# Squared-ReLU attention and two MLPs on one core: GpSimd's elementwise work moved to VectorE, and the square taken in fp32 on ScalarE

## The chip, the cores and the metric

The kernel runs on one core of a Trainium2 chip. The metric is the device time in microseconds (us) of one execution; smaller is better.

## The reference

For each of 2 batches of 3008 rows, `scores = (z @ z.T) / S`, `attn = max(scores, 0)**2`, `out = u * (attn @ v)`, with `z` 64 wide and `u`, `v` 256 wide. The 6016 rows that result go through two MLPs of inner width 2048:

```python
h = x @ w_in                      # first MLP
P = a[0] + a[1]*h + a[2]*h**2 + a[3]*h**3
Q = 1 + abs(b[0])*abs(h) + abs(b[1])*h**2
x = (P / (Q + 1e-6)) @ w_out
h = x @ moe2_w_in                 # second MLP
out = max(0.01*h, h) @ moe2_w_out
```

All four weight matrices are float64; the kernel reads each element as two 32-bit words and builds one fp32 number from them.

## The kernel before, in words

Every product is made of three matmuls: an operand is split into a rounded copy in fp32r (the high part) and the remainder (the low part), and high x high, low x high and high x low are accumulated.

The 6016 rows lie in 12 blocks, six for each batch: five of 512 columns and one of 448 (block 5 and block 11). A block has 12 steps, each with two tiles of 128 keys, so attention is 144 steps, `t`. In step `t` TensorE does 4 matmuls of scores (`scores`, L224) and 12 of attention times V for the step two before it (`av(t - 2)`, L257); in the second step of a block 10. The score tiles `big` are two deep, the squares' tiles three (`r`, `ph`) and two (`pl`).

The order on every engine is written out by hand (`manual_schedule`), and each engine works strictly in that order. In step `t` it is:

- ScalarE: ReLU of the scores into `r` (L226), then the square of `r` rounded to fp32r, `ph` (L228).
- VectorE: `square(t)`, the square of `r` in place in fp32 (L232); `square_low(t)`, `r - ph` into `pl` (L238). The last of the 144 goes to GpSimd.
- Then the tasks of the step. `prep_v` (chunks of V, five in steps 2 to 10, six in steps 64 to 74): ScalarE rounds a chunk (L173) and the remainder is taken on GpSimd (L175), for the first chunk on VectorE. `prep_z` (steps 1, 6, 64, 68, 76): TensorE transposes, ScalarE rounds the keys (L141), VectorE takes their remainder (L142). `prep_u` (tenth step of a block): TensorE transposes (L207), ScalarE copies. At a block's end VectorE multiplies with `u` (L262).
- Weights: 32 halves, one begun every 3.4 steps, in steps 2 to 113 (`load_w`, `conv1` to `conv5`, one a step). `conv1`: ScalarE takes the absolute value of the upper word (L287) and GpSimd clamps it (L288). `conv2`, `conv3`, `conv4`: VectorE shifts and masks (L294), joins an exponent bit and the sign (L298, L299), and joins the lower word (L303). `conv5`: ScalarE rounds (L315), GpSimd takes the remainder (L316), and for the second MLP's weights SyncE stores both to DRAM (L318).

All DMAs are issued by SyncE, in order. From step 119 the first chunks of the first MLP run between the attention steps (the merged stretch, to about 612 us); after it TensorE goes through the rest of both MLPs, with no work on GpSimd.

Of the kernel before, what the change touches and what calls it, by code (L numbers as in the profile page):

```python
# [10 lines left out]
F32R = mybir.dt.float32r  # L11
I32 = mybir.dt.int32
AF = mybir.ActivationFunctionType
ALU = mybir.AluOpType
# [3 lines left out]
def f32(ap):  # L18
    return ap.bitcast(F32)
# [3 lines left out]
def squared_relu_attention_moe_moe2(  # L23
# [14 lines left out]
    pe, act, dve, pool, sp = nc.tensor, nc.scalar, nc.vector, nc.gpsimd, nc.sync  # L38
# [9 lines left out]
    NPAIR = KB // 2  # L48
# [3 lines left out]
    blocks = []  # L52
# [9 lines left out]
    def slot(i, name, dt=F32, shape=(P, 2, QB)):  # L62
        return sb.tile(list(shape), dt, tag=f"s{i}", name=name)

    def big(name):
        return ps.tile([P, 2, QB], F32, tag="big", name=name)
# [10 lines left out]
    def rtile(i, name):  # L77
        return sb.tile([P, 2, 1024], F32R, tag=f"r{i}", name=name)
# [4 lines left out]
    C0 = 1.0 + 1e-6  # L83
    LSH = 2.0 ** -63
    par = sb.tile([P, 16], F32, tag="par", name="par")
    F64_LEAST, F64_MOST = 2.0 ** -15, 122879.9921875
    lnb, exb = par[:, 12:13], par[:, 13:14]

# [24 lines left out]
    extra_t = sb.tile([P, 2, 1024], F32, tag="r2", name="extra")  # L113
# [5 lines left out]
    def key_chunk(c):  # L119
        return keys[c // 2][:, c % 2, :]  # L120
# [48 lines left out]
    def prep_v(b, c, t):  # L169
        m = rtile(3 + c, f"V{b}_{c}")  # L170
        V[b, c] = m
        tf = t.rearrange("p k d -> p (k d)")
        act.activation(m[:, 0, :], tf, AF.Copy)  # L173
        eng = pool if b or c else dve
        eng.tensor_tensor(out=m[:, 1, :], in0=tf, in1=f32(m[:, 0, :]), op=ALU.subtract)  # L175
        if c == KB // 4 - 1:
            o = 3 * D
            act.activation(m[:KTAIL, 1, o:], f32(m[:KTAIL, 0, o:]), AF.Copy)
            pool.memset(f32(m[KTAIL:, 0, o:]), 0.0)
# [33 lines left out]
    R, PH, PL = {}, {}, {}  # L213

    def scores(t):
        i, pr = divmod(t, NPAIR)
        b, q0, n = blocks[i]
        s = big(f"sc{t}")
        for e in range(2):
            kb = 2 * pr + e  # L220
            o = (kb % 8) * P
            m = key_chunk(kb // 8)[:, o : o + P]
            for h in range(2):
                pe.matmul(s[:, e, :n], m, queries[i % 2][:, h, :n], start=h == 0, stop=h == 1)  # L224
        r = (extra[0] if t % 3 == 2 else slot(t % 3, f"r{t}"))[:, :, :n]
        act.activation(r, s[:, :, :n], AF.Relu, scale=SCALE)  # L226
        ph = slot(4 + t % 3, f"ph{t}", F32R)[:, :, :n]
        act.activation(ph, r, AF.Square)  # L228
        PH[t], R[t] = ph, r

    def square(t):
        dve.tensor_tensor(out=R[t], in0=R[t], in1=R[t], op=ALU.mult)  # L232

    def square_low(t):
        r, ph = R.pop(t), PH[t]
        pl = slot(7 + t % 2, f"pl{t}", F32R)[:, :, : blocks[t // NPAIR][2]]
        eng = pool if t == NT - 1 else dve
        eng.tensor_tensor(out=pl, in0=r, in1=f32(ph), op=ALU.subtract)  # L238
        PL[t] = pl

    def av(t):
        i, pr = divmod(t, NPAIR)
        b, q0, n = blocks[i]
        if pr == 0:
            pacc[i] = acc(own_acc(i), f"oT{i}")
        a = pacc[i]
        ph, pl = PH.pop(t), PL.pop(t)
        seq = [(0, ph), (1, ph), (0, pl)]
        for si, (h, mv) in enumerate(seq):
            for e in range(2):  # L250
                kb = 2 * pr + e
                if kb == KB - 1 and si == 0:
                    continue
                vt = V[b, kb // 4]
                for j in range(2):
                    o = (kb % 4) * D + j * P
                    pe.matmul(a[:, j, :n], vt[:, h, o : o + P], mv[:, e, :],  # L257
                              start=pr == 0 and si == 0 and e == 0,
                              stop=pr == NPAIR - 1 and si == 2 and e == 1)
        if pr == NPAIR - 1:  # L260
            xt = uT.pop(i)[:, :, :n]
            dve.tensor_tensor(out=xt, in0=xt, in1=pacc.pop(i)[:, :, :n], op=ALU.mult)  # L262
            if i < NB - 1:
                at(t + DEPTH + 2, lambda: sp.dma_start(xs[i], xt))
            else:
                sp.dma_start(xs[i], xt)
# [5 lines left out]
    conv = {}  # L272

    def load_w(k):
# [7 lines left out]
            sp.dma_start(t.rearrange("p (k d) w -> p k (d w)", k=2), src[r0 : r0 + 256, :].rearrange("(k p) w -> p k w", p=P))  # L282
        conv[k] = t

    def conv1(k):
        c = slot(15, f"cvc{k}", I32)[:, 0, :]
        act.activation(f32(c), f32(conv[k][:, :, 1]), AF.Abs)  # L287
        pool.tensor_scalar(out=f32(c), in0=f32(c), scalar1=F64_LEAST, scalar2=F64_MOST, op0=ALU.max, op1=ALU.min)  # L288
        conv["c"] = c

    def conv2(k):
        c = conv["c"]
        conv["a", k] = a = extra_t[:, 1, (k % 2) * 512 : (k % 2 + 1) * 512].bitcast(I32)
        dve.tensor_scalar(out=a, in0=c, scalar1=3, scalar2=0x3FFFFFF8, op0=ALU.logical_shift_left, op1=ALU.bitwise_and)  # L294

    def conv3(k):
        c, a, raw = conv["c"], conv["a", k], conv[k]
        dve.scalar_tensor_tensor(out=a, in0=c, scalar=0x40000000, in1=a, op0=ALU.bitwise_and, op1=ALU.bitwise_or)  # L298
        dve.scalar_tensor_tensor(out=a, in0=raw[:, :, 1], scalar=-0x80000000, in1=a, op0=ALU.bitwise_and, op1=ALU.bitwise_or)  # L299

    def conv4(k):
        a, raw = conv["a", k], conv.pop(k)
        dve.scalar_tensor_tensor(out=a, in0=raw[:, :, 0], scalar=29, in1=a, op0=ALU.logical_shift_right, op1=ALU.bitwise_or)  # L303

    def conv5(k):
        kind, j, half = halves[k]
        a = conv.pop(("a", k))
        cols = slice(half * 512, (half + 1) * 512)
        if kind < 2:
            if half == 0:  # L310
                W[kind, j] = sb.tile([P, 2, 1024], F32R, tag=f"w{kind}_{j}", name=f"w{kind}_{j}")
            w = W[kind, j][:, :, cols]
        else:
            w = slot(9, f"wst{k}", F32R)
        act.activation(w[:, 0, :], f32(a), AF.Copy)  # L315
        pool.tensor_tensor(out=w[:, 1, :], in0=f32(a), in1=f32(w[:, 0, :]), op=ALU.subtract)  # L316
        if kind >= 2:
            sp.dma_start(w2s[kind, j][:, :, cols], f32(w))  # L318

# [6 lines left out]
    NT = NB * NPAIR  # L326
# [109 lines left out]
    def m1_h(c):  # L436
        i, p = divmod(c, NP)
        T[c] = {"n": blocks[i][2], "h": hidden(f"h1_{c}", 0, p, X1[i], blocks[i][2])}
# [5 lines left out]
    def m1_tb(c):  # L444
        if c % 2 and c <= MERGED:
            T[c]["t1"] = extra[1][:, :, : T[c]["n"]]
        else:
            m1_tile(c, "t1", 13 if c % 2 else 2)
        act.activation(T[c]["t1"], T[c]["h"], AF.Abs, scale=b0)  # L449

    def m1_s(c):
        act.activation(m1_tile(c, "t2", 7 if c > NP and c % 2 else 3), T[c]["h"], AF.Square)  # L452

    def m1_v(c):
        act.activation(m1_tile(c, "t3", 12 if c % 2 else 10), T[c]["h"], AF.Identity, scale=ca[3], bias=ca[2])
# [5 lines left out]
    def m1_w(c):  # L461
        d = T[c]
        dve.tensor_tensor(out=d["t3"], in0=d["t3"], in1=d["h"], op=ALU.mult)
        dve.scalar_tensor_tensor(out=d["t3"], in0=d["t3"], scalar=ca[1], in1=d["h"], op0=ALU.add, op1=ALU.mult)  # L464
# [21 lines left out]
    def m1_y(c, parts):  # L486
        i, p = divmod(c, NP)
        if p == 0 and 0 in parts:
            Y1[i] = acc(1, f"y1_{i}")
        d = T[c]  # L490
        project(Y1[i], 1, p, d["gh"], d["gl"] if 2 in parts else None, d["n"], parts)
        if 2 in parts:
            T.pop(c)
# [95 lines left out]
    for t in range(NT + DEPTH):  # L589
        c, ph = divmod(t - m0, 3)  # L590
        c = c if t >= m0 and c < MERGED else None
        if t < NT:
            scores(t)
        if c is not None and ph == 0:
            m1_h(c)
        if c and ph == 1:
            m1_y(c - 1, (0, 1, 2))
        if t >= DEPTH:
            av(t - DEPTH)
        if t < NT:  # L600
            square(t)
        if c is not None and ph == 0:
            m1_tb(c)
            m1_s(c)
            m1_v(c)
            m1_w(c)
            m1_q(c)
        if t < NT:
            square_low(t)
        for f in tasks.pop(t, []):  # L610
            f()
        if c is not None and ph == 1:
            m1_r(c)
            if c == NP:
                split_x2(0)
            m1_gh(c)
            m1_back(c)
        if c is not None and ph == 2:
            m1_gl(c)
# [97 lines left out]
```

## Time and profile before

| | us |
|---|---|
| median of 3 runs | 1607.09 (1605.28 to 1607.85) |
| the profiled execution, its own time | 1606.98 |
| its span, first to last instruction | 1605.2 |
| TensorE busy in the span | 1581.3 |
| VectorE busy in the span | 1438.3 |
| ScalarE busy in the span | 1098.6 |
| GpSimd busy in the span | 165.4 |

The times are in us from the span's start. The span is 1.8 us shorter than the execution's own time. A busy share is an average over stages with different limits, so the views below are taken by stretches that begin and end where a block's first scores begin.

### The profile page before, as it was taken

Reading aid. Unit: us, or ns where it says so; the run is one execution under the profiler, and the core shown is the slowest. Engines: PE = TensorE matmul, PEld = TensorE weight load, DVE = VectorE, ACT = ScalarE, POOL = GpSimd, SP = SyncE. Lnnn points to the kernel's source line nnn. Section 1 sums busy time; section 2 is a strip of 40 time slices with the busy share of each in tenths; the row PEclk is TensorE's granted clock in tenths of the full one; section 3 lists DMA queues with packets and bytes.
Section 4 is the critical chain, followed back from the end, with each engine's and each line's share of the span. In section 5 each row is a group of like instructions: output and inputs, shape, how many; then the busy total and the mean of one; then the engine's idle time right before and its main releaser. Section 6 shows DMA issues by size and latency. Waiting matters only on the chain.

```text
span 1605.2 us, 17951 instructions
## 1 busy us (share of the span) xinstructions
PE 1581.3 (99%) x7140; PEld 1323.7 (82%) x7140; DVE 1438.3 (90%) x1231; ACT 1098.6 (68%) x1109; POOL 165.4 (10%) x86
## 2 busy tenths in 40 slices
PE   8999999999999999999999999999999999999998
PEld 6788888788878887888888888888888888888887
DVE  7999999999979989999999998899999999999852
ACT  6666666666667766677777677777767676777643
POOL 2433335433200000000000000000000000000000
PEclk9999999999999999999999999999999999999999
DMA  6223236343220132000000000000000000000000
GB/s 170 66 67 87 84 90 178 115 137 119 92 68 23 56 113 104 13 14 14 14 1 12 13 13 14 13 14 13 12 14 14 13 14 1 25 1 0 14 1 25
DMA packets 51555, 74.42 MB, mean 46 GB/s; under 512 B 15632, under 2 KB 35344, under 8 KB 50448
## 3 DMA queue, kind: packets, MB, share of 16 engines
q1 hardware_dynamic: 51472, 73.28, 14.8%
q8 instruction: 56, 0.92, 0.2%
q14 instruction: 27, 0.22, 0.0%
HBM read 46.93 MB, written 20.71 MB: 42 GB/s over the span
## 4 chain that ended last, share of the span: by engine, by line
PE 85%; DVE 11%; issue 2%; ACT 2%; DMA 1%; DVEq 0%; POOL 0%; POOLq 0%; ACTq 0%
PE h L418 31%; PE y L432 31%; PE oT L257 16%; PE sc L224 5%; DVE pl L238 3%; DVE r L232 2%; DVE extra L232 1%; PE y L538 1%; DVE extra L303 1%; DVE extra L299 0%; PE uTp L207 0%; DVE t L464 0%; DVE extra L298 0%; DVE keys L142 0%; DVE t L459 0%
## 5 line engine op out<-in xcount | busy, mean ns | idle before, releaser
L432 PE MATMUL y<-gh,w 128*128 128x512 f32 (+1 forms) x1536 | 374.2, 386 | 0.7 <-DVE gh L475 0.5
L432 PEld LDWEIGHTS y<-gh,w 128*128 128x128 f32 x1536 | 288.2, 188 | 55.0 <-PE h L418 0.9
L257 PE MATMUL oT<-ph,V 128*128 128x512 f32 (+1 forms) x1128 | 276.3, 387 | 0.0
L257 PEld LDWEIGHTS oT<-ph,V 128*128 128x128 f32 x1128 | 212.9, 189 | 40.4
L432 PE MATMUL y<-gl,w 128*128 128x512 f32 (+1 forms) x768 | 203.3, 386 | 2.1 <-DVE gl L514 1.9
L418 PE MATMUL h<-x2h,w 128*128 128x512 f32 (+1 forms) x768 | 204.1, 388 | 0.0
L507 ACT ACTIVATE gh<-h 128x1024 fp32r<-128x1024 f32 (+1 forms) x96 | 97.0, 1011 | 143.1 <-PE y L432 125.1
L449 ACT ACTIVATE t<-h,par 128x1024 f32<-128x1024 f32 (+1 forms) x91 | 100.1, 1100 | 128.9 <-PE h L418 128.8
L432 PEld LDWEIGHTS y<-gl,w 128*128 128x128 f32 x768 | 144.1, 188 | 30.4 <-DVE gl L514 2.3
L418 PEld LDWEIGHTS h<-x2h,w 128*128 128x128 f32 x768 | 144.2, 189 | 26.2
L257 PE MATMUL oT<-pl,V 128*128 128x512 f32 (+1 forms) x576 | 153.7, 389 | 7.2 <-DVE pl L238 6.8
L459 DVE SCALAR_TENSOR_TENSOR t<-t,par,t 128x1024 f32<-128x1024 f32 (+1 forms) x91 | 114.6, 1259 | 46.0 <-ACT t L452 46.0
L238 DVE TENSOR_TENSOR pl<-r,ph 128x1024 fp32r<-128x1024 f32 (+1 forms) x96 | 139.7, 1455 | 9.1
L514 DVE TENSOR_TENSOR gl<-g,gh 128x1024 fp32r<-128x1024 f32 (+1 forms) x96 | 114.9, 1197 | 29.5 <-ACT g L509 29.5
L257 PEld LDWEIGHTS oT<-pl,V 128*128 128x128 f32 x576 | 107.1, 188 | 32.8 <-DVE pl L238 13.4
L468 ACT ACTIVATE t<-t,par 128x1024 f32<-128x1024 f32 (+1 forms) x91 | 103.4, 1136 | 36.9 <-DVE t L459 36.9
L475 DVE SCALAR_TENSOR_TENSOR gh<-t,par,t 128x1024 fp32r<-128x1024 f32 (+1 forms) x91 | 114.7, 1260 | 15.3 <-PE y L432 3.0
L226 ACT ACTIVATE r<-sc 128x1024 f32<-128x1024 f32 (+1 forms) x96 | 96.3, 1003 | 46.8 <-PE sc L224 45.1
L232 DVE TENSOR_TENSOR r<-r 128x1024 f32<-128x1024 f32 (+1 forms) x96 | 120.5, 1255 | 3.9 <-ACT ph L228 3.9
L483 DVE SCALAR_TENSOR_TENSOR t<-t,par,t 128x1024 f32<-128x1024 f32 (+1 forms) x96 | 121.1, 1262 | 3.1
L464 DVE SCALAR_TENSOR_TENSOR t<-t,par,h 128x1024 f32<-128x1024 f32 (+1 forms) x96 | 120.8, 1259 | 3.4
L418 PE MATMUL h<-x1h,w 128*128 128x512 f32 (+1 forms) x448 | 117.4, 384 | 2.7 <-DVE t L464 2.5
(92 smaller groups left out, 2468.9 us busy)
## 6 DMA issues: line engine op xcount, KB each, us to landing
wraw<-in_moe_w_in_dram SPq DMA_DIRECT2D x16, 512.0 KB, 4.9
wraw<-in_moe_w_out_dram SPq DMA_DIRECT2D x16, 512.0 KB, 4.1
w2s<-wst SPq DMA_DIRECT2D x16, 512.0 KB, 3.7
w<-w2s SPq DMA_DIRECT2D x8, 1024.0 KB, 4.9
vraw<-in_v_dram SPq DMA_DIRECT2D x10, 512.0 KB, 6.1
u<-in_u_dram SPq DMA_DIRECT2D x10, 512.0 KB, 5.2
xs<-u SPq DMA_DIRECT2D x10, 512.0 KB, 4.4
out_dram<-yo SPq DMA_DIRECT2D x10, 512.0 KB, 2.9
```

The lines of the kernel that those rows point to most:

```text
L232: dve.tensor_tensor(out=R[t], in0=R[t], in1=R[t], op=ALU.mult)
L238: eng.tensor_tensor(out=pl, in0=r, in1=f32(ph), op=ALU.subtract)
L257: pe.matmul(a[:, j, :n], vt[:, h, o : o + P], mv[:, e, :], start=pr == 0 and si == 0 and e == 0, stop=pr == NPAIR - 1 and si == 2 and e == 1)
L418: pe.matmul(h[:, e, :n], w[:, hl, o : o + P], mv[:, k, :n], start=si == 0 and k == 0, stop=si == 2 and k == 1)
L432: pe.matmul(a[:, j, :n], w[:, hl, o : o + P], mv[:, e, :], start=p == 0 and si == 0 and e == 0, stop=p == NP - 1 and si == 2 and e == 1)
L449: act.activation(T[c]["t1"], T[c]["h"], AF.Abs, scale=b0)
L459: dve.scalar_tensor_tensor(out=d["t2"], in0=d["t2"], scalar=b1, in1=d["t1"], op0=ALU.mult, op1=ALU.add)
L464: dve.scalar_tensor_tensor(out=d["t3"], in0=d["t3"], scalar=ca[1], in1=d["h"], op0=ALU.add, op1=ALU.mult)
L468: act.activation(d["t1"], d["t2"], AF.Ln, scale=LSH, bias=lnb)
L475: dve.scalar_tensor_tensor(out=m1_tile(c, "gh", 14, F32R), in0=d["t3"], scalar=ca[0], in1=d["t1"], op0=ALU.add, op1=ALU.mult)
L483: dve.scalar_tensor_tensor(out=d["t3"], in0=d["t3"], scalar=ca[0], in1=d["t2"], op0=ALU.add, op1=ALU.subtract)
L514: dve.tensor_tensor(out=d["gl"], in0=d["g"], in1=f32(d["gh"]), op=ALU.subtract)
```

## The change

- `prep_v` and `conv5` take every remainder on VectorE.
- `scores` squares `r` in place in fp32 on ScalarE; `square` on VectorE goes, and `square_high`, a copy of `r` rounded to fp32r on VectorE, stands in its place. `square_low` is on VectorE for the last step too.
- The clamp goes from `conv1` to `conv2`, on VectorE. With the upper word scaled by 65536 on ScalarE (L287's place), the shift and mask (now `conv3`) do what two joins did: one of the three `scalar_tensor_tensor` of a half goes, and the sign's moves to `conv4`.
- Only two small memsets of V's tail, those of the parameters and the identity's making stay on GpSimd.

```diff
+    TWO16 = 65536.0
@@ prep_v
-        eng = pool if b or c else dve
-        eng.tensor_tensor(out=m[:, 1, :], in0=tf, in1=f32(m[:, 0, :]), op=ALU.subtract)
+        dve.tensor_tensor(out=m[:, 1, :], in0=tf, in1=f32(m[:, 0, :]), op=ALU.subtract)
@@ scores
-        ph = slot(4 + t % 3, f"ph{t}", F32R)[:, :, :n]
-        act.activation(ph, r, AF.Square)
-        PH[t], R[t] = ph, r
-
-    def square(t):
-        dve.tensor_tensor(out=R[t], in0=R[t], in1=R[t], op=ALU.mult)
+        act.activation(r, r, AF.Square)
+        R[t] = r
+
+    def square_high(t):
+        PH[t] = slot(4 + t % 3, f"ph{t}", F32R)[:, :, : blocks[t // NPAIR][2]]
+        dve.tensor_copy(out=PH[t], in_=R[t])
@@ square_low
-        eng = pool if t == NT - 1 else dve
-        eng.tensor_tensor(out=pl, in0=r, in1=f32(ph), op=ALU.subtract)
+        dve.tensor_tensor(out=pl, in0=r, in1=f32(ph), op=ALU.subtract)
@@ conv1 to conv4
-        act.activation(f32(c), f32(conv[k][:, :, 1]), AF.Abs)
-        pool.tensor_scalar(out=f32(c), in0=f32(c), scalar1=F64_LEAST, scalar2=F64_MOST, op0=ALU.max, op1=ALU.min)
+        act.activation(f32(c), f32(conv[k][:, :, 1]), AF.Abs, scale=TWO16)
...
     def conv2(k):
         c = conv["c"]
+        dve.tensor_scalar(out=f32(c), in0=f32(c), scalar1=F64_LEAST * TWO16, scalar2=F64_MOST * TWO16, op0=ALU.max, op1=ALU.min)
+
+    def conv3(k):
+        c = conv["c"]
         conv["a", k] = a = extra_t[:, 1, (k % 2) * 512 : (k % 2 + 1) * 512].bitcast(I32)
-        dve.tensor_scalar(out=a, in0=c, scalar1=3, scalar2=0x3FFFFFF8, op0=ALU.logical_shift_left, op1=ALU.bitwise_and)
-
-    def conv3(k):
-        c, a, raw = conv["c"], conv["a", k], conv[k]
-        dve.scalar_tensor_tensor(out=a, in0=c, scalar=0x40000000, in1=a, op0=ALU.bitwise_and, op1=ALU.bitwise_or)
-        dve.scalar_tensor_tensor(out=a, in0=raw[:, :, 1], scalar=-0x80000000, in1=a, op0=ALU.bitwise_and, op1=ALU.bitwise_or)
+        dve.tensor_scalar(out=a, in0=c, scalar1=3, scalar2=0x7FFFFFF8, op0=ALU.logical_shift_left, op1=ALU.bitwise_and)
 
     def conv4(k):
         a, raw = conv["a", k], conv.pop(k)
+        dve.scalar_tensor_tensor(out=a, in0=raw[:, :, 1], scalar=-0x80000000, in1=a, op0=ALU.bitwise_and, op1=ALU.bitwise_or)
         dve.scalar_tensor_tensor(out=a, in0=raw[:, :, 0], scalar=29, in1=a, op0=ALU.logical_shift_right, op1=ALU.bitwise_or)
@@ conv5
-        pool.tensor_tensor(out=w[:, 1, :], in0=f32(a), in1=f32(w[:, 0, :]), op=ALU.subtract)
+        dve.tensor_tensor(out=w[:, 1, :], in0=f32(a), in1=f32(w[:, 0, :]), op=ALU.subtract)
@@ the step
-            square(t)
+            square_high(t)
```

## Rows read from the trace of the kernel before

**Rows 1.** Part 1 of the page: busy us (share of the span) x instructions.
```profile
PE 1581.3 (99%) x7140; PEld 1323.7 (82%) x7140; DVE 1438.3 (90%) x1231; ACT 1098.6 (68%) x1109; POOL 165.4 (10%) x86
```

**Rows 2.** Windows: stretch, its length, busy us (x instructions), granted clock, DMA share, GB/s.
```profile
core 0: us, PE busy (x) PEld busy (x) DVE busy (x) ACT busy (x) POOL busy (x), PEclk, DMA share, GB/s
11.22:54.24 43.02, 39.71 (x180) 31.39 (x178) 41.93 (x29) 30.66 (x34) 20.50 (x11) 1.00 0.40 115
54.24:100.30 46.06, 45.26 (x200) 36.18 (x198) 44.64 (x43) 31.62 (x35) 17.44 (x8) 1.00 0.26 81
100.30:144.26 43.96, 43.96 (x200) 36.49 (x198) 42.02 (x41) 29.84 (x32) 14.60 (x7) 1.00 0.25 72
107.10:144.26 37.16, 37.16 (x170) 30.86 (x168) 35.46 (x34) 25.09 (x28) 11.79 (x6) 1.00 0.29 86
...
232.18:280.74 48.56, 45.89 (x215) 40.34 (x214) 46.98 (x40) 32.71 (x39) 25.63 (x12) 0.93 0.64 178
280.74:329.42 48.68, 45.89 (x207) 36.95 (x206) 47.27 (x42) 32.04 (x36) 19.02 (x10) 1.00 0.42 122
...
457.58:529.05 71.47, 70.49 (x313) 57.30 (x312) 66.05 (x57) 52.53 (x51) 0.00 (x0) 1.00 0.07 22
...
585.07:611.70 26.63, 22.55 (x100) 18.01 (x98) 21.07 (x19) 14.57 (x15) 2.13 (x1) 1.00 0.19 66
```

**Rows 3.** Timeline, TensorE in block 5: start, us, line, operation, tiles [idle before <-releaser].
```profile
238.84 0.97 PE L224 MATMUL sc<-keys,keys 128*128 128x448 f32 x4
...
242.08 0.98 PE L224 MATMUL sc<-keys,keys 128*128 128x448 f32 x4
...
242.90 1.78 PE L257 MATMUL oT<-ph,V 128*128 128x448 f32 x8
...
272.08 1.07 PE L257 MATMUL oT<-pl,V 128*128 128x448 f32 x4 [2.48 <-DVE pl L238]
...
276.87 3.19 PE L257 MATMUL oT<-ph,V 128*128 128x448 f32 x8
```

**Rows 4.** Waits, whole span: who waited for whom, us in total, times, longest.
```profile
ACT wst L315 <- DVE extra L303: 21.0, 14, 4.9
...
PE oT L257 <- DVE pl L238: 6.8, 8, 2.5
...
ACT cvc L287 <- DMA wraw<-in_moe_w_in_dram: 6.1, 2, 4.6
...
PE h L418 <- DVE t L464: 2.5, 1, 2.5
...
PE sc L224 <- DVE keys L142: 2.2, 1, 2.2
...
PE h L418 <- DVE x1l L398: 1.7, 2, 1.2
```

**Rows 5.** Timeline, GpSimd and VectorE from 42 to 48 us.
```profile
42.48 2.48 POOL L175 TENSOR_TENSOR V<-vraw,V 128x1024 fp32r<-128x1024 f32 x1 [0.16 <-ACT V L173]
42.62 3.42 DVE L232 TENSOR_TENSOR extra<-extra 128x1024 f32<-128x1024 f32 x1
...
44.91 2.28 POOL L316 TENSOR_TENSOR w<-extra,w 128x512 fp32r<-128x512 f32 x1
...
46.15 2.13 DVE L238 TENSOR_TENSOR pl<-extra,ph 128x1024 fp32r<-128x1024 f32 x1
```

**Rows 6.** VectorE's lines: count, duration ns min/median/max, first and last start.
```profile
L238 DVE TENSOR_TENSOR pl<-r,ph x96: 1091/1225/3281, 12.4 to 586.3; 128x1024 fp32r<-128x1024 f32 x80, 128x896 fp32r<-128x896 f32 x16
...
L232 DVE TENSOR_TENSOR r<-r x96: 1077/1217/3426, 11.1 to 585.1; 128x1024 f32<-128x1024 f32 x80, 128x896 f32<-128x896 f32 x16
...
L294 DVE TENSOR_SCALAR extra<-cvc x32: 412/416/2630, 31.6 to 432.1; 128x512 int32<-128x512 int32 x32
...
L299 DVE SCALAR_TENSOR_TENSOR extra<-wraw,extra x32: 691/692/2781, 38.7 to 435.7; 128x512 int32<-128x512 int32 x32
```

**Rows 7.** Groups by form: VectorE's copies, both from PSUM (busy us, mean ns).
```profile
L558 DVE COPY yt<-y 128x448 f32<-128x448 f32 x1 | 0.6, 625 | 5.1 <-ACT yt L557 5.1
L572 DVE COPY to<-yf 128x256 f32<-128x256 f32 x1 | 0.4, 423 | 1.4 <-ACT to L566 1.4
```

## The prediction

> **What bounds the kernel now.** I read the busy times first [rows 1]: TensorE is busy in 99% of the span, so a faster VectorE can win only where TensorE stands still or repeats work slowly. The 24 us that are missing from the span's 1605.2 us are to be found, so I read the windows next, cut at the blocks' first scores [rows 2]. From 100.30 to 144.26 us a block takes 43.96 us with TensorE busy throughout: this is the floor of a block of 512 columns (12 steps of 3.63 us, one of them two matmuls short, and one set of transposes). VectorE is busy for 42.02 us of it, which costs nothing there. Four attention stretches are longer than their floor:
>
> - Steps 2 to 11, 11.22 to 54.24 us: 43.02 us. The same steps of an undisturbed block, 107.10 to 144.26 us, take 37.16 us; here `prep_z` adds one more set of 8 transposes, about 0.8 us. Floor 37.96 us, loss 5.1 us.
> - Block 1, 54.24 to 100.30 us: 46.06 us against 43.96 us, loss 2.1 us.
> - Block 5, 232.18 to 280.74 us: a step of 448 columns takes 3.24 us (the scores at 238.84 and 242.08 us [rows 3]). The first two steps, which still carry block 4's products, end at 238.84 us after 6.66 us; ten of 3.24 us and three sets of transposes (2.4 us) give a floor of 41.5 us. Measured 48.56 us, loss 7.1 us.
> - Block 6, 280.74 to 329.42 us: two steps with products of 448 columns (0.29 us shorter each), one more set of transposes, so 43.96 - 0.58 + 0.8 = 44.2 us. Measured 48.68 us, loss 4.5 us.
>
> Together 18.8 us. The waits [rows 4] say who ends last there: TensorE waits for `pl` of `square_low` and for the keys' remainder, both VectorE. The lost time is more than the waits' sum, because after the wait of 2.48 us at 272.08 us TensorE runs for some microseconds at the lower of its two clock levels, 1.2 for 2.4 GHz: eight matmuls take 3.19 us where they took 1.78 us, and the granted clock of block 5 is 0.93 [rows 2, 3].
>
> Why VectorE is late shows in the timeline [rows 5]: while GpSimd takes V's remainder for 2.48 us, VectorE's square takes 3.42 us instead of 1.22 us; during the weights' remainder `square_low` takes 2.13 us. The medians are 1.217 and 1.225 us, the longest over 3.2 us, and the same holds for the short conversions, 0.416 us at the median and up to 2.63 us [rows 6]. One engine waits until the other's instruction is over. The losses lie where `prep_v` runs, steps 2 to 10 and 64 to 74, and just after.
>
> The Trainium skill has this too (SBUF — State Buffer, the section on the two sides of SBUF): the port pair that GpSimd shares with VectorE is an exclusive lock, and a VectorE instruction with two SBUF inputs can be blocked by GpSimd's whole instruction. The trace agrees (3.42 us over a GpSimd instruction of 2.48 us). By the rule all such excess goes with GpSimd's work.
>
> **The change part by part.** *Square.* VectorE's 1.217 us becomes a copy of 1024 elements from SBUF, rounded. The trace has no such copy; two rows bound it. The copies from PSUM [rows 7] take 625 ns for 448 elements and 423 ns for 256: 1.05 ns an element and 0.154 us fixed, so 1.23 us for 1024. The `tensor_scalar` from SBUF to SBUF [rows 6] takes 0.416 us for 512, which after the same fixed part is 0.51 ns an element: 0.68 us for 1024, 0.61 us for 896. One input, SBUF on both sides and 4-byte elements make the copy most like the latter; I take 0.68 us and keep 1.23 us as the other bound.
>
> On this the Trainium skill is explicit (VectorE: DVE Perf Modes, the perf-mode tier table): an fp32 copy or `tensor_scalar` within SBUF runs at twice the rate, from PSUM it does not, and `tensor_tensor` never does in fp32. It gives 1227 ns for 2048 elements; an estimate from that for 1024 is 0.69 us. No run here yet shows it for an fp32r output. The same page (rules for kernel authors) speaks against the change: keep the number of VectorE instructions low. By count VectorE gets 44 more (32 clamps, 32 weight remainders, 11 of V and one `square_low`, less 32 joins); at 0.154 us fixed each that alone would be 6.8 us more of VectorE, where the sum by durations below comes out lower than before.
>
> *ScalarE* squares in the same place for the same length, and its absolute value takes a scale: no change. What waits there is the same as before: `square_high(t)` stands behind ScalarE's square as `square(t)` did. New is that the high products of `av(t)` need VectorE. They begin two steps (7.3 us) later: no cost while VectorE is less than a step behind.
>
> *Weights.* A half costs VectorE 0.416 + 3 x 0.692 = 2.5 us now. After: clamp and shift at 0.416 us, two joins and the remainder at 0.692 us [rows 6], 2.9 us, in steps already spaced. ScalarE now waits for the last join (21.0 us for one kind of half [rows 4]) because VectorE is late; the remainder queues behind ScalarE's rounding copy, but `square_high` and `square_low` stand before it, 1.9 us of work. SyncE's store behind the remainder, and the next weight load behind that, come no later than from GpSimd.
>
> *V.* Eleven remainders at 1.23 us (the `tensor_tensor` median) move to VectorE.
>
> *Sums.* A step is 0.68 + 1.225 = 1.9 us of VectorE (1.7 us at 448 columns), a block has 12 / 3.4 = 3.5 halves. An undisturbed block: 22.9 + 3.5 x 2.9 + 1.2 (product with `u`) = 34.3 us against 43.96 us. The tight stretches:
>
> - Steps 2 to 11: 19.0 + five V remainders 6.1 + keys 1.2 + two halves and a little 6.2 = 32.5 us, floor 37.96 us.
> - The ten 448-column steps of block 5: 17.0 + four V 4.9 + two keys 2.5 + 2.9 halves 8.5 = 32.9 us, floor 34.8 us.
> - Block 6: 22.9 + two V 2.5 + keys 1.2 + halves 10.3 + product 1.2 = 38.1 us, floor 44.2 us.
>
> All fit. `pl` has room for more than one step of delay, so bursts pass. In block 5 only 2 us are to spare and VectorE must also stand still for ScalarE now and then: I leave 1.5 us of the 18.8 us lost, and recover 17.3 us. With the waits the half-speed stretch goes.
>
> *Merged stretch.* GpSimd is idle there, so only the copy helps, 0.54 us a step. TensorE's idle time is 0.98 us from 457.58 to 529.05 us, and 4.08 us from 585.07 to 611.70 us [rows 2]. The waits for `x1l` and `gl` lie behind squares: I recover 0.8 us, and 0.7 us of the longest wait for `x1l`, 1.2 us [rows 4]. The 2.5 us wait for L464 follows from VectorE's chain after the last step, where no square is left; it stays. The last `square_low`, now on VectorE, falls behind L459 into a gap before `x2l`: nothing, or 1.1 us if the gap closes. Later stages have none of the changed instructions.
>
> Sum: 17.3 + 1.5 = 18.8 us off the profiled execution's 1606.98 us, 1588.2 us. That execution is within 0.1 us of the median, 1607.09 us.
>
> **The rivals.**
>
> 1. *The copy runs at 1.23 us.* For it: both copies in the trace do. Against: they read PSUM. The three tight stretches then hold 38.0, 37.4 and 44.7 us of VectorE against 37.96, 34.8 and 44.2 us: 3.1 us over, and with bursts some 6.5 us of the losses stay; the merged stretch gains nothing. 1606.98 - 18.8 + 6.5 = 1595 us.
> 2. *Half the losses come from late data.* For it: in block 5 the DMA engines are 0.64 busy, and ScalarE waits 6.1 us for weights. Against: TensorE's waits name VectorE. If half of 18.8 us stays and nothing is won after, 1606.98 - 9.4 = 1598 us. If all stays, the change doesn't do what it is for: 1607 us.
> 3. *Slower: VectorE waits in its own queue.* Each remainder now stands in front of the next step's square. If VectorE stood still for 3.3 us a half (for ScalarE), 3.5 halves are 11.6 us a block. Undisturbed blocks have 9.7 us to spare, so seven of them lose 1.9 us each, 13.3 us; the tight stretches have 5.5, 1.9 and 6.1 us to spare against 2.1, 2.9 and 3.5 halves (6.9, 9.6 and 11.6 us) and lose 14.6 us. 1606.98 - 18.8 + 27.9 = 1616 us. It decides from about 3.1 us a half. Against: 1.9 us of work stand before each remainder, and ScalarE is busy for 30 of 44 us [rows 2].
>
> **How the numbers follow.** Chances: the forecast 0.73, with its own range 1584 to 1592 us (all of the 18.8 us and the merged stretch's waits gone, or 4 us left); the copy at single rate 0.12; half from late data 0.10, all of it 0.03; slower 0.02. The range that leaves out no more than 2 in 10 reaches from 1583 us, where part of the wait for L464 goes as well, to 1598 us, rivals 1 and 2. Under 0.2%, about 3 us, this kernel's times can't be told apart (its three runs span 2.6 us). Faster: 0.95; same 0.03; slower 0.02.
>
> **What would show it.** The copy group at 0.68 us or 1.23 us. The squares' remainder with a maximum near 1.23 us, not 3.28 us. The first block's steps 2 to 11 at 38 us, block 5 near 42 to 43 us at a granted clock of 1.00, block 6 near 44 us. VectorE's busy time down by some 90 us (0.54 us less a step in 144 steps is 78 us, the rest the end of the blocking less the added work), and GpSimd's to a few us. Wrong: waits of TensorE for `ph` from the copy, VectorE idle before the weights' or V's remainder for more than 2 us a time, or a new half-speed stretch of TensorE.

## The result, and the profile after

The changed kernel takes 1588.54 us (median of 4 runs, 1587.2 to 1589.0), the kernel before 1606.77 us: a ratio of 0.9886, 95% interval 0.9869 to 0.9903. The forecast was 1588.2 us. The profiled execution took 1589.0 us with a span of 1587.2 us; before it was 1606.98 and 1605.2 us.

Part 1 of the page, which answers to [rows 1]: busy us (share of the span) x instructions.

```profile
PE 1573.4 (99%) x7140; PEld 1322.7 (83%) x7140; DVE 1337.4 (84%) x1275; ACT 1098.3 (69%) x1109; POOL 1.6 (0%) x10
```

VectorE has 44 instructions more and is busy for 100.9 us less. The windows, cut at the same steps as [rows 2] (length, busy us of each engine, granted clock, DMA share, GB/s):

```profile
10.88:49.09 38.21, 38.21 (x179) 31.78 (x178) 33.43 (x38) 30.59 (x34) 0.31 (x1) 1.00 0.45 133
49.09:93.05 43.96, 43.96 (x199) 36.50 (x198) 32.92 (x43) 31.81 (x35) 0.00 (x0) 1.00 0.28 84
93.05:137.01 43.96, 43.96 (x199) 36.50 (x198) 33.05 (x43) 29.63 (x32) 0.00 (x0) 1.00 0.25 74
224.93:267.20 42.27, 42.27 (x215) 38.16 (x214) 37.36 (x49) 32.51 (x39) 0.00 (x0) 1.00 0.73 200
267.20:311.55 44.35, 44.35 (x207) 37.32 (x206) 36.46 (x47) 32.46 (x38) 0.47 (x1) 1.00 0.48 138
439.71:510.06 70.35, 70.16 (x314) 57.36 (x311) 59.55 (x56) 52.87 (x51) 0.00 (x0) 1.00 0.07 22
```

In all five attention windows TensorE's busy time equals the length: nothing is lost any more. Against [rows 2] the four disturbed stretches give back 4.81, 2.10, 6.29 and 4.33 us, together 17.5 us. From the first step of the merged stretch to the last step of attention (439.71 to 566.07 us, before 457.58 to 585.07 us) it is 1.1 us less, the start 0.3 us less, and what follows the last attention step takes 1.0 us more. That is the span's 18.0 us.

VectorE's lines, for [rows 6] (count, duration ns min/median/max, first and last start):

```profile
L232 DVE CAST ph<-r x96: 619/694/696, 10.7 to 565.6; 128x1024 fp32r<-128x1024 f32 x80, 128x896 fp32r<-128x896 f32 x16
...
L237 DVE TENSOR_TENSOR pl<-r,ph x96: 1091/1226/1228, 11.4 to 566.7; 128x1024 fp32r<-128x1024 f32 x80, 128x896 fp32r<-128x896 f32 x16
...
L299 DVE TENSOR_SCALAR extra<-cvc x32: 419/420/428, 33.2 to 415.6; 128x512 int32<-128x512 int32 x32
```

The copy (the trace calls it CAST) takes 0.694 us at the median, the double rate. Of these lines no instruction is longer than its median by more than 0.01 us, where the remainder of the square went up to 3.28 us and the shift up to 2.63 us [rows 6].

The 1.0 us that the end loses, in the timeline of TensorE (start, us, line, operation, tiles, wait before):

```profile
592.33 1.16 PE L419 MATMUL h<-x1h,w 128*128 128x512 f32 x4 [2.52 <-DVE t L465]
593.33 0.84 PE L419 MATMUL h<-x1l,w 128*128 128x512 f32 x2
593.96 1.91 PE L419 MATMUL h<-x1h,w 128*128 128x512 f32 x4
595.67 1.05 PE L419 MATMUL h<-x1l,w 128*128 128x512 f32 x2
596.52 2.23 PE L433 MATMUL y<-gh,w 128*128 128x512 f32 x8
```

and in the window behind the wait (columns as above):

```profile
593.50:597.00 3.50, 3.50 (x10) 2.69 (x10) 3.33 (x4) 0.66 (x2) 0.00 (x0) 0.51 0.51 211
```

After the wait for L465 (the L464 of before) four matmuls take 1.91 us instead of 1.09, eight 2.23 us instead of 1.98. The granted clock is 0.51 from 593.50 to 597.00 us, the lower level, 1.2 GHz; this is worth 1.7 us over the last four of the groups shown. In the profiled execution of the kernel before, the same wait of 2.5 us had no such stretch behind it. It comes and goes from execution to execution, as the last section shows.

### The profile page after: what moved, and what is told of

The parts are those of the page before. It is cut to its first block, busy times and chain, and to the rows that moved or that the text cites. A ratio compares the mean times of both kernels' runs of the same rounds, so it can differ in the third digit from the quotient of the medians.

```text
span 1587.2 us, 17867 instructions
## 1 busy us (share of the span) xinstructions
PE 1573.4 (99%) x7140; PEld 1322.7 (83%) x7140; DVE 1337.4 (84%) x1275; ACT 1098.3 (69%) x1109; POOL 1.6 (0%) x10
## 4 chain that ended last, share of the span: by engine, by line
PE 96%; DVE 2%; ACT 1%; DMA 0%; issue 0%; SPq 0%; DVEq 0%; ACTq 0%
PE h L419 32%; PE y L433 32%; PE oT L256 23%; PE sc L224 8%; PE uTp L207 1%; PE y L539 1%; DMA zraw<-in_z_dram 0%; PE zT L136 0%; DVE t L465 0%; DVE t L460 0%; DVE t L464 0%; DVE pl L237 0%; SPq L127 0%; DVE gh L476 0%; ACT t L456 0%
## 5 line engine op out<-in xcount | busy, mean ns | idle before, releaser
L464 DVE TENSOR_TENSOR t<-t,h 128x1024 f32<-128x1024 f32 (+1 forms) x96 | 114.5, 1193 | 14.5 <-ACT t L456 14.5
L237 DVE TENSOR_TENSOR pl<-r,ph 128x1024 fp32r<-128x1024 f32 (+1 forms) x96 | 115.5, 1204 | 10.1 <-PE oT L256 0.9
L465 DVE SCALAR_TENSOR_TENSOR t<-t,par,h 128x1024 f32<-128x1024 f32 (+1 forms) x96 | 120.9, 1259 | 3.4
```

What stands on the lines that cost most here:

```text
L237: dve.tensor_tensor(out=pl, in0=r, in1=f32(ph), op=ALU.subtract)
```

## The experiments

Two theories went into the runs. **The whole time:** TensorE loses where VectorE's own work and its blocking by GpSimd together exceed TensorE's time for longer than the two steps that the tiles can hold. **Blocking alone:** each VectorE instruction that GpSimd blocks puts TensorE back. Lengths of the four stretches in us, from the windows of each run's profiled execution, beside the median of all executions. Run again beside the experiments, the kernel before took 1606.6 to 1607.2 us; the ratios below are to these:

| kernel | median | steps 2-11 | block 1 | block 5 | block 6 |
|---|---|---|---|---|---|
| before | 1606.77 | 43.02 | 46.06 | 48.56 | 48.68 |
| changed | 1588.54 | 38.21 | 43.96 | 42.27 | 44.35 |
| square only | 1594.37 | 38.24 | 43.99 | 42.78 | 49.52 |
| moves only | 1598.81 | 39.48 | 44.67 | 42.27 | 50.34 |
| copy with two inputs | 1599.86 | 39.66 | 45.14 | 42.23 | 51.11 |
| V back on GpSimd | 1591.92 | 38.18 | 43.97 | 42.28 | 48.20 |
| weights back on GpSimd | 1587.59 | 38.22 | 43.96 | 42.28 | 44.44 |
| GpSimd writes only | 1590.84 | 38.15 | 43.96 | 42.27 | 44.35 |
| V alone moved | 1603.60 | 40.53 | 48.44 | 43.96 | 50.08 |
| moves, loads earlier | 1594.97 | 39.44 | 44.62 | 42.27 | 48.46 |
| moves, V's tail later | 1596.53 | 39.60 | 43.96 | 42.28 | 48.90 |
| end of merged stretch reordered | 1583.07 | 38.20 | 43.96 | 42.27 | 44.73 |

**The square alone**, in the kernel before; GpSimd keeps its work.

```diff
-        ph = slot(4 + t % 3, f"ph{t}", F32R)[:, :, :n]
-        act.activation(ph, r, AF.Square)
-        PH[t], R[t] = ph, r
+        act.activation(r, r, AF.Square)
+        R[t] = r
...
-            square(t)
+            square_high(t)
```

> The kernel before with the change of the square alone (fp32 square on ScalarE, rounded copy on VectorE); all of GpSimd's work stays. Theory (VectorE's whole time in the tight stretches decides: own work and blocking together): a step has 0.53 us less of VectorE, so steps 2 to 11, block 5 and block 6 hold about 36.6, 42 and 41 us of VectorE against floors of 38, 41.5 and 44.2 us; 2 to 5 us of the 18.8 us stay, and the merged stretch gains its 1 to 2 us: 1590 to 1594 us. Rival (blocking by GpSimd alone costs the time, each blocked instruction on TensorE's path): blocked instructions stay above 3 us and at least 12 of the 18.8 us stay: 1599 us or more.

Measured 1594.37 us (ratio 0.9919, 0.9904 to 0.9934). Instructions are still blocked; `square_low` takes up to 3.24 us:

```profile
L238 DVE TENSOR_TENSOR pl<-r,ph x96: 1091/1226/3237, 11.7 to 572.3; 128x1024 fp32r<-128x1024 f32 x80, 128x896 fp32r<-128x896 f32 x16
```

Yet three of the four stretches stand within about 0.5 us of the changed kernel's, so blocking alone falls. The theory of the whole time has the size, 0.4 us above its range, but not the place. It had put the loss into block 5 (42 us of VectorE against a floor of 41.5 us). Nearly all of what stays, 5.2 us, lies in block 6, where VectorE is busy for 41.64 us, less than the 44.35 us of the floor. There ScalarE waits 6.4 us for GpSimd's remainder of V (3.9 and 2.5 us) and 4.8 us for one weight.

**The moves alone**, and **the copy with two inputs**: the changed kernel with the old square, and with `max(r, r)` for the copy. The edit shown is that of the second; the first undoes the square's part of the change.

```diff
-        dve.tensor_copy(out=PH[t], in_=R[t])
+        dve.tensor_tensor(out=PH[t], in0=R[t], in1=R[t], op=ALU.max)
```

> The changed kernel with the square as before (rounded square on ScalarE, fp32 square on VectorE at 1.22 us); GpSimd's work is on VectorE. Theory of the whole time: by my sums the tight stretches hold 38.0, 37.4 (of 34.8) and 44.7 us of VectorE, so about 6 us of the losses stay, most of it in block 5, and the merged stretch gains nothing: 1593 to 1597 us. Rival (blocking alone): no blocking is left, so all of the attention stretch's 18 us comes: 1589 to 1590 us.

> The changed kernel with the rounded copy written as max(r, r) of two inputs, 1.22 us instead of 0.69 us; the same result, and TensorE's high products still wait for VectorE. It measures my first rival, the copy at single rate, priced at 1595 us (1593 to 1597 us). If the high products' new wait for VectorE costs nothing, it equals the kernel with the moves alone within 2 us; if it costs, it is slower than that one by more.

Measured 1598.81 us (0.9946, 0.9929 to 0.9962) and 1599.86 us (0.9955, 0.994 to 0.997). That something stays was right and blocking alone is refuted, for nothing is blocked in either (the longest square, copy or `square_low` takes 1.228 us); but both are 2 to 3 us above the range expected, and not where I had put it: block 5 stands at its floor and block 6 loses 6 to 7 us. The two differ by 1 us, so TensorE's new dependence on VectorE for the high products costs about 1 us even where VectorE is late. Alone, the square wins 12.8 us and the moves 8.4 us; together they win 18.2 us, less than the sum.

**V's remainders back on GpSimd**, in the changed kernel.

```diff
-        dve.tensor_tensor(out=m[:, 1, :], in0=tf, in1=f32(m[:, 0, :]), op=ALU.subtract)
+        eng = pool if b or c else dve
+        eng.tensor_tensor(out=m[:, 1, :], in0=tf, in1=f32(m[:, 0, :]), op=ALU.subtract)
```

> The changed kernel with V's eleven remainders back on GpSimd. Theory of the whole time: VectorE loses 1.2 us of own work and gets some 2 us of blocking for each, so steps 2 to 11 hold 36 us of 38, block 5 about 36 us of 34.8 in its ten steps: 0 to 2 us lost against the changed kernel, 1588 to 1591 us. Rival (blocking alone): each of eleven blocked instructions puts TensorE back by about 1 us: 1597 us or more.

Measured 1591.92 us (0.9904, 0.9889 to 0.9919), 3.4 us above the changed kernel and 0.9 us above the range expected. In the profiled execution block 6 is 3.9 us longer and no other stretch. The timeline shows how, from engine to engine (ScalarE is ACT):

```profile
281.43 2.44 POOL L176 TENSOR_TENSOR V<-vraw,V 128x1024 fp32r<-128x1024 f32 x1 [6.82 <-ACT V L174]
281.71 3.23 DVE L238 TENSOR_TENSOR pl<-extra,ph 128x1024 fp32r<-128x1024 f32 x1
...
283.90 0.42 ACT L179 ACTIVATE V<-V 64x256 fp32r<-64x256 f32 x1 [2.55 <-POOL V L176]
...
286.35 0.69 DVE L233 CAST ph<-r 128x1024 fp32r<-128x1024 f32 x1 [1.07 <-ACT r L228]
```

GpSimd blocks `square_low` for 2 us; ScalarE stands for 2.55 us in its fixed order for the same remainder, and then VectorE stands for ScalarE's square.

**The weights back on GpSimd**, in the changed kernel.

```diff
-        dve.tensor_scalar(out=f32(c), in0=f32(c), scalar1=F64_LEAST * TWO16, scalar2=F64_MOST * TWO16, op0=ALU.max, op1=ALU.min)
+        pool.tensor_scalar(out=f32(c), in0=f32(c), scalar1=F64_LEAST * TWO16, scalar2=F64_MOST * TWO16, op0=ALU.max, op1=ALU.min)
...
-        dve.tensor_tensor(out=w[:, 1, :], in0=f32(a), in1=f32(w[:, 0, :]), op=ALU.subtract)
+        pool.tensor_tensor(out=w[:, 1, :], in0=f32(a), in1=f32(w[:, 0, :]), op=ALU.subtract)
```

> The changed kernel with the weights' 32 clamps and 32 remainders back on GpSimd; V's remainders stay on VectorE. VectorE has 1.1 us less of its own work a half and gets blocked for up to 2.5 us a half. Theory of the whole time in the tight stretches, as the run with V's remainders on GpSimd corrected it (3.4 us lost, 3.9 us of it in block 6): undisturbed blocks stay at 43.96 us, block 6 loses 0 to 3 us: 1588 to 1592 us. Rival (each blocked instruction reaches TensorE): 32 halves with some 0.3 us each or more, 1598 us or more.

Measured 1587.59 us (0.9888, 0.9873 to 0.9903), 0.4 us below the range expected and the same as the changed kernel (0.9886). Blocking is there, and harmless:

```profile
L237 DVE TENSOR_TENSOR pl<-r,ph x96: 1091/1226/2198, 11.1 to 566.1; 128x1024 fp32r<-128x1024 f32 x80, 128x896 fp32r<-128x896 f32 x16
```

So with the copy at double rate, moving the weights' clamp and remainder won nothing that these runs can show; V's remainders and the square did.

**GpSimd writes only.** The kernel before, its low parts of V (from the second chunk) and of the weights replaced by zeros, its clamp left out.

```diff
-        eng.tensor_tensor(out=m[:, 1, :], in0=tf, in1=f32(m[:, 0, :]), op=ALU.subtract)
+        if eng is dve:
+            dve.tensor_tensor(out=m[:, 1, :], in0=tf, in1=f32(m[:, 0, :]), op=ALU.subtract)
+        else:
+            pool.memset(f32(m[:, 1, :]), 0.0)
...
-        pool.tensor_scalar(out=f32(c), in0=f32(c), scalar1=F64_LEAST, scalar2=F64_MOST, op0=ALU.max, op1=ALU.min)
...
-        pool.tensor_tensor(out=w[:, 1, :], in0=f32(a), in1=f32(w[:, 0, :]), op=ALU.subtract)
+        pool.memset(f32(w[:, 1, :]), 0.0)
```

> The kernel before, with GpSimd's remainders of V and of the weights replaced by memsets of the same tiles and its clamps left out: the low parts of V (from the second chunk on) and of all weights are zero, the clamp is not computed. GpSimd still holds its places in the order but reads nothing from SBUF; VectorE's work is that of the kernel before. If it is the reading that blocks VectorE's instructions of two inputs: the maxima of the squares fall to 1.23 us, VectorE's clean load fits every stretch, the attention blocks go to their floors and the merged stretch keeps its losses: 1588 to 1591 us. Rival (GpSimd's place in the order, its late finishes, or its writing cost the time): 1598 us or more, and long squares remain.

Measured 1590.84 us (0.9907, 0.9892 to 0.9921), in the range expected, and every stretch at its floor, with VectorE's square at 1.22 us as before. VectorE's 1231 instructions are busy for 1386.2 us where they were for 1438.3 us. The memsets are shorter than the remainders (0.53 and 0.95 us for some 1.5 and 2.7 us), wait for less and partly run earlier, so their places are not the old ones. Still, 28 two-input instructions of VectorE overlap them, and none of these is longer than 1.227 us. The only long one is a single-input instruction at double rate, once, behind four memsets in a row:

```profile
L241 DVE TENSOR_TENSOR pl<-r,ph x96: 1091/1226/1228, 13.2 to 569.8; 128x1024 fp32r<-128x1024 f32 x80, 128x896 fp32r<-128x896 f32 x16
...
L296 DVE TENSOR_SCALAR extra<-cvc x32: 418/420/1691, 29.0 to 414.7; 128x512 int32<-128x512 int32 x32
```

The run leaves two things together: with the long remainders, ScalarE's waits for them are gone too. In block 6 of the kernel before ScalarE waits 6.0 us for GpSimd's remainder of V (3.1 and 2.9 us), here not at all. So GpSimd's long instructions make the losses of the kernel before, but how much came by way of VectorE's blocked instructions, and how much by results that reached ScalarE late, is not shown.

**V's remainders alone moved**, in the kernel before.

```diff
-        eng = pool if b or c else dve
-        eng.tensor_tensor(out=m[:, 1, :], in0=tf, in1=f32(m[:, 0, :]), op=ALU.subtract)
+        dve.tensor_tensor(out=m[:, 1, :], in0=tf, in1=f32(m[:, 0, :]), op=ALU.subtract)
```

> The kernel before with V's eleven remainders alone moved to VectorE. VectorE gives 1.22 us of its own for some 2 us of blocking each, about 9 us less over steps 2 to 10 and 64 to 74. Theory of the whole time: half or less of the 18.8 us comes, for the clean load with the weights still blocking is 38 us in steps 2 to 11 and over the floor in block 5: 1598 to 1603 us. Rival (V's blocking alone is the cause): 14 us or more, 1593 us or less.

Measured 1603.60 us (0.9977, 0.9967 to 0.9987), 0.6 us above the range: a sixth of the gain. Blocks 1 and 6 are even longer than before, block 1 with a stretch at the lower clock in it (granted 0.96). The weights' blocking, harmless beside the double-rate copy, is not harmless where the square takes 1.22 us: with the weights moved as well (the moves alone) the time is some 5 us less.

**Why block 6 keeps losing.** With the moves alone VectorE comes late into block 6: from a step's first scores to the end of its `square_low` it takes 5.9 us in the first step of block 5 and 9.2 us in the first of block 6 (4.9 and 5.3 us in the changed kernel). In block 6 ScalarE then waits (us in total, times, longest):

```profile
ACT cvc L289 <- DMA wraw<-in_moe_w_in_dram: 6.4, 1, 6.4
ACT V L178 <- DVE V L175: 5.5, 1, 5.5
```

Two runs, both from the kernel with the moves alone, aim at one wait each: weight loads one step earlier, and the copy of V's last rows two steps later.

```diff
-        for dt, f in ((-1, load_w), (1, conv1), (2, conv2), (3, conv3), (4, conv4), (5, conv5)):
+        for dt, f in ((-2, load_w), (1, conv1), (2, conv2), (3, conv3), (4, conv4), (5, conv5)):
```

```diff
         if c == KB // 4 - 1:
-            o = 3 * D
-            act.activation(m[:KTAIL, 1, o:], f32(m[:KTAIL, 0, o:]), AF.Copy)
-            pool.memset(f32(m[KTAIL:, 0, o:]), 0.0)
+            at(step + 2, lambda: v_tail(m))
...
```

> The kernel with the moves alone (square as before, GpSimd's work on VectorE), which loses 8 us in attention, 6.1 us of them in block 6, and each weight load issued one step earlier. ScalarE stood for 6.4 us in its queue for one weight there, and VectorE for 2.4 us behind it. If late weights stop VectorE through ScalarE's queue: that wait goes and block 6 takes 47 to 49 us instead of 50.3: 1595 to 1598 us. If VectorE's own load is all of it: no change, block 6 within 0.5 us, 1598 to 1600 us.

> The same kernel with the moves alone, and the copy of V's last rows on ScalarE put two steps later; it stood for 5.5 us in ScalarE's queue for VectorE's remainder of V, and VectorE for 2.1 us behind it. If the two engines' waits for each other in their fixed order make the rest of the loss: block 6 takes 47.5 to 49 us, 1595 to 1598 us. If VectorE's own load is all of it: block 6 within 0.5 us of 50.3 us, 1598 to 1600 us.

Measured 1594.97 us (0.9929, 0.9913 to 0.9946) and 1596.53 us (0.9938, 0.9923 to 0.9953); block 6 takes 48.46 and 48.90 us instead of 50.34, as expected if the waits count. The two edits win 1.9 and 1.4 us of the 6 us: through a late load and through the tail's copy VectorE's lateness comes back to VectorE by way of ScalarE's queue. The second does not take its wait away cleanly, for ScalarE then stands 11.1 us for two weights in block 6 instead of 6.4 us for one. And of the first run's gain in the profiled executions, 4.6 us, 2.9 us lie behind the last attention step, where that of the moves alone has two stretches at the lower clock and this one none. The two edits were not tried together; what is left of the 6 us is not settled.

**The end of the merged stretch reordered**, in the changed kernel: three instructions of VectorE take other places.

```diff
+        if pr == NPAIR - 1 and i == NB - 1:
+            return
...
-    at(m0 + 3 * NP - 1, lambda: split_x1_low(1))
...
+        if t == m0 + 3 * NP - 1:
+            split_x1_low(1)
         if t < NT:
             square_low(t)
...
-            m1_r(c)
             if c == NP:
                 split_x2(0)
+            m1_r(c)
...
         m1_w(c)
+        if c == MERGED:
+            last_product()
```

> The changed kernel with three instructions of VectorE moved at the end of the merged stretch: the low part of x1 of block 1 ahead of the last but one square_low, the split of the first MLP output ahead of the logarithm and exponential of the ninth chunk, and the last product with u behind the next chunk's two products. If VectorE's chain there is what TensorE still waits for: the waits of 0.8, 0.6 and 2.5 us before TensorE's h and y shrink to under 1 us together and the stretch at the lower clock after them goes: 3 to 5 us less than the changed kernel, 1583.5 to 1585.5 us. Rival (the chain through ScalarE's logarithm and exponential sets the end): within 1.5 us of the changed kernel.

Measured 1583.07 us (1582.84 to 1583.65; 0.9857, 0.9841 to 0.9874), 5.5 us below the changed kernel and 0.4 us below the range expected. One wait of 0.54 us is left of three, and the matmuls behind it keep their pace:

```profile
589.57 1.17 PE L425 MATMUL h<-x1h,w 128*128 128x512 f32 x4 [0.54 <-DVE t L471]
...
591.03 1.07 PE L425 MATMUL h<-x1h,w 128*128 128x512 f32 x4
```

The chain of VectorE was the cause there, as expected; which of the three moves counts was not separated. Not all of the 5.5 us is theirs. The changed kernel's profiled execution has two stretches at the lower clock after attention, behind this wait and near 1540 us, and this one has neither. Beside the execution of the weights back on GpSimd, which has neither as well, what follows the last attention step is 3.5 us shorter (1014.8 against 1018.3 us). This version beats both kernels.

## Why the prediction was right

- **Where the time was.** 18.8 us of loss in four stretches; 17.5 us came back and TensorE's floors show that no more was there. My floor of block 5 was 0.8 us too low (41.5 against 42.27 us), so "1.5 us stay" was right in sum for a wrong reason.
- **The copy** at 0.68 us: 0.694 us. VectorE in an undisturbed block: 34.3 us forecast, 33.05 us measured; steps 2 to 11: 32.5 and 33.43 us.
- **The merged stretch**: 0.8 us forecast up to the last step, 1.1 us measured; of the wait for `x1l` after it 0.7 us forecast, 0.6 us measured (from 1.2 to 0.6 us).
- **What I did not count**: the new stretch at the lower clock, 1.7 us. I had named such a stretch as a sign against me and given it no price. Without it the span would have fallen by 19.7 us, 0.9 us more than the sum. So it is partly luck that the median lies within 0.4 us of the forecast: what the sum left out on either side nearly cancels.
- **The mechanism.** That GpSimd's remainders lengthen VectorE's two-input instructions, and that memsets in their place don't, is shown by the run in which GpSimd only writes: VectorE's busy time falls by 52 us and every stretch goes to its floor. That VectorE's lateness by this blocking made all of the 18.8 us is not shown, since ScalarE's waits for GpSimd went with it. That blocking costs only where there is no room for it is shown by the square alone and by the weights back on GpSimd, where blocked instructions stay and nothing, or only block 6, is lost.
- **The first rival was mispriced.** At 1.22 us the copy gives 1599.86 us, not 1595 us, so "6.5 us of the losses stay" was too low. The step that failed there was the tally by stretch: I charged each stretch what VectorE had too much in it. But the tiles carried block 5's lateness into block 6, where V's last chunk and a late weight stopped ScalarE's queue and with it VectorE. The tally found the load, not the place, and had no term for two engines that wait for each other in fixed orders.
- **Late data** alone cost nothing: in the changed kernel block 5 runs at its floor at a DMA share of 0.73, and block 6 too, though ScalarE waits 4.9 us for one weight in it. Beside a late VectorE it does cost, as the run with earlier loads shows; how much of the losses before the change it made was not tried.

## What to carry to other kernels

Find the floor of a repeated stretch in an undisturbed repetition and charge the losses by stretch; an engine that is 96% busy beside the bound costs nothing there and decides everything where a burst comes. Before work leaves GpSimd, add up VectorE's own time with the blocking: parts that win little (V's remainders 3 us in the kernel before, the weights nothing in the changed one) belong to a whole that wins 18 us with a square at half the price. And where several engines follow fixed orders, look past the load at what stands behind a late instruction in the next queue.

## What the runs showed of the hardware

- Beside GpSimd's memsets VectorE's two-input instructions kept their length (1.228 us at most), while a `tensor_scalar` at double rate once took 1.691 us instead of 0.420; beside GpSimd's remainders, which read, two-input instructions took up to 3.43 us. The Trainium skill (SBUF — State Buffer, Summary: rules for kernel authors) says this: a VectorE instruction with two SBUF inputs contends with a GpSimd instruction that reads SBUF, one in a two-port mode with any, and the second to start stands until the first is over. The runs agree on which instructions meet.
- A copy from fp32 to fp32r within SBUF runs at double rate, 0.694 us for 1024 elements, as the perf-mode tier table of the Trainium skill (VectorE: DVE Perf Modes) has it for fp32.
- The same wait of TensorE for `t`, 2.52 to 2.54 us, stands in eleven of the profiled executions. Right behind it five ran on at 1.2 GHz (the changed kernel, the square alone, the copy with two inputs, GpSimd writes only, V's tail later; granted clock 0.50 to 0.51), and six at 2.4 GHz (granted clock 1.00). In the changed kernel the stretch cost 1.7 us. Such a wait can thus cost two thirds as much again, or nothing; what decides is open. Single runs of one kernel differ too: of the four with the weights back on GpSimd, two have a granted clock of 1.000 over the span (1585.86 and 1586.71 us) and two of 0.997 and 0.998 (1590.76 and 1588.48 us).

On how long one engine stands for the other, the runs agree with that rule of the Trainium skill for the remainders and not for the clamp, which reads too. In the kernel before, 71 two-input instructions of VectorE overlap clamps alone, and none is longer than its median by more than 0.44 us; beside V's remainders it is up to 2.2 us, beside the weights' 0.92 us. A square that starts 1.03 us into a clamp is over before it:

```profile
96.00 2.89 POOL L288 TENSOR_SCALAR cvc<-cvc 128x512 f32<-128x512 f32 x1
97.03 1.63 DVE L232 TENSOR_TENSOR r<-r 128x1024 f32<-128x1024 f32 x1
```

The measurement decides: the prediction's "waits until the other's instruction is over" holds for the remainders only, and the clamps, 82.7 of GpSimd's 165.4 us, blocked little.
